# Layer norm in halves, products sorted by kind, earlier score blocks, and maxima negated where they are taken

## The chip, the cores and the metric

The kernel runs on one core of one Trainium2 chip. The metric is the device time of that core in microseconds (us); three runs of the kernel before gave 1825.66 to 1826.9 us, with a median of 1826.27 us.

## The reference

The input x is 2048 tokens of 512 numbers. It is normed, and the normed tokens go through an attention of 32 heads of width 16 and through a feed-forward net; the net's output gates the attention's. The weights wo and those of the net are drawn at random too.

```python
xn = (x - mean(x)) / sqrt(var(x) + 1e-5)
q, k, v = split(xn @ wqkv)                 # 32 heads of 16
p = softmax(q @ k.T * 16 ** -0.5)          # per head, 2048 x 2048
s = (p @ v) @ wo
g = silu(((xn @ w_gate) * (xn @ w_up)) @ w_down)
out = x + s * g
```

## The kernel before, in words

**Precision.** Every product is made of three: each operand is split into a high part in fp32r and a low part, and high times high, high times low and low times high are summed in one PSUM bank.

**Early stage** (`early`, up to 118.5 us). The 16 token tiles of 128 are normed in four chunks of four tiles. A chunk takes statistics on DVE (L161, L162), the root on DVE and ACT (L166, L167), six tiny DVE operations (L171 to L176) that give the scale e and the offset mr, the application (L183 on DVE for tiles 0 and 1, L185 on ACT for the others), and per tile a "turn": four PE transposes into one bank of tag "x" (L192), the high part copied out by ACT (L195), the low part subtracted on DVE (L196). POOL splits the weights wk and wq (L132 cast, L133 subtract) and subtracts the low parts of the V weights.

PE then works through a stream of 264 "products" (a product is one matmul with 512 columns; 12 make one result of k, q or v). The list `gens` gives their order: k of chunk 0, q of chunk 0, V tiles 0 and 1, k of chunk 1, and so on. A finished k or q bank is cast by ACT (L262), its low part is subtracted on DVE (L266), and both are stored to DRAM (KD, QD) and loaded again into `ks` and `qs` in the layout of the heads, all through the queue of SP. Results of k, q and V share two banks of tag "f". The table in `early` says at which product number each piece of the norm of chunks 1 to 3 is issued; the list EARLY says at which product numbers a score block stands. A score block is four matmuls s (L512) and four DVE maxima over 512 keys (L514), in four banks of tag "s". There are 21 of them.

**Rounds** (512, from 118.5 us on). A unit is four heads and 512 queries; it has 16 rounds of 128 keys. A round has four matmuls t (L538, scores with the row maximum subtracted, through two extra rows of `qs`), whose exponentials ACT takes (L540), four matmuls s with their maxima for the unit 21 rounds later (L512, L514), a portion of "filler" (projections, feed-forward net, last product), and the four pv matmuls of the round before (L549).

**Maxima.** When a unit's 64 partial maxima per row are there, `maxima` reduces them on DVE to m (L518), writes -m rounded to fp32r into one half of mm (L521), and two steps of the round's loop later (four steps make a round) writes the rest, -m minus that, into the other half (L524), transposes mm (L526) and sends it through DRAM (MD) into the two extra rows of `qs`. The unit's first t needs them; that is six rounds after `maxima`. There are 32 of them; the first is taken in the early stage, with no steps between.

**Order.** PE, ACT and DVE run in the order in which the program is written. POOL and the queue of SP are ordered by the scheduler.

Of the kernel before, what the change touches and what calls it, by code (L numbers as in the profile page):

```python
# [34 lines left out]
SPLIT_ROUNDS = 4  # L35
EBUFS = 12
HBUFS = 2
EARLY = [66 + 9 * n for n in range(21)]
EARLY_BUFS = {"s": 4, "x": 2, "f": 2}
BUFS = {"st": 2, "s": 3, "pv": 1, "misc": 2}  # L40
LOWER, UPPER = slice(0, 64), slice(64, P)
# [4 lines left out]
def body(ctx, tc, x, wqkv, wo, wg, wu, wd, out):  # L46
# [4 lines left out]
    def dma(dst, src):  # L51
        nc.sync.dma_start(dst, src)
# [45 lines left out]
    def soon(n, fn):  # L98

        if n:  # L100
            waiting.append((steps[0] + n, fn))
        else:
            fn()

# [20 lines left out]
    def wtile(name):  # L125
        return keep.tile([P, ND, P], F32 if name[-1] == "r" else F32R, name=name, bufs=1 if name[-1] == "r" else 2)

    def split(name, src):

        raw, hi, lo = [wtile(name + n) for n in "rhl"]  # L130
        dma(raw, src.rearrange("(d p) f -> p d f", p=P))
        nc.gpsimd.tensor_copy(hi, raw)  # L132
        nc.gpsimd.tensor_tensor(lo, raw, hi, op=OP.subtract)  # L133
        return hi, lo

# [16 lines left out]
    def load_x(tt):  # L152
        dma(tokens(tt), x[tt * P:(tt + 1) * P])

    def ln_stats(tt):
        c, t = divmod(tt, 4)
        if t == 0:
            norm[c] = [qp.tile([P, 4, 2], F32, name="mv", bufs=2)] + [qp.tile([P, 4], F32, name=n, bufs=2)
                                                                        for n in ("ve", "r0", "e1", "mr")]
        st = qp.tile([P, 6], F32, name="st", bufs=2)  # L160
        nc.vector.bn_stats(st, tokens(tt))  # L161
        nc.vector.bn_aggr(norm[c][0][:, t], st)  # L162

    def ln_root(c):
        mv, ve, r0, e, mr = norm[c]
        nc.vector.tensor_scalar(ve, mv[:, :, 1], 1e-5, None, op0=OP.add)  # L166
        nc.scalar.activation(r0, ve, AF.Sqrt)  # L167

    def ln_scale(c):
        mv, ve, r0, e, mr = norm[c]  # L170
        nc.vector.reciprocal(r0, r0)  # L171
        nc.vector.tensor_tensor(e, r0, r0, op=OP.mult)
        nc.vector.tensor_tensor(e, e, ve, op=OP.mult)
        nc.vector.tensor_scalar(e, e, -0.5, 1.5, op0=OP.mult, op1=OP.add)
        nc.vector.tensor_tensor(e, r0, e, op=OP.mult)
        nc.vector.scalar_tensor_tensor(mr, mv[:, :, 0], -1.0, e, op0=OP.mult, op1=OP.mult)  # L176

    def ln_apply(tt):
        c, t = divmod(tt, 4)
        mv, ve, r0, e, mr = norm[c]  # L180
        xt = tokens(tt)
        if tt < 2:
            nc.vector.tensor_scalar(xt, xt, e[:, t:t + 1], mr[:, t:t + 1], op0=OP.mult, op1=OP.add)  # L183
        else:
            nc.scalar.activation(xt, xt, AF.Identity, bias=mr[:, t:t + 1], scale=e[:, t:t + 1])  # L185

    def ln_turn(tt):
        c, t = divmod(tt, 4)
        xt = tokens(tt)
        pt = psum("x", f"xT{tt}")  # L190
        for d in range(ND):
            nc.tensor.transpose(pt[:, d * P:(d + 1) * P], xt[:, d * P:(d + 1) * P], ident)  # L192
        ptv = pt.rearrange("p (d q) -> p d q", d=ND)
        sl = slice(t * P, (t + 1) * P)
        nc.scalar.activation(xh[c][:, :, sl], ptv, AF.Copy)  # L195
        nc.vector.tensor_tensor(xl[c][:, :, sl], ptv, xh[c][:, :, sl], op=OP.subtract)  # L196


    def mm3(o, lh, ll, rh, rl, first, last):
        nc.tensor.matmul(o, lh, rh, start=first, stop=False)  # L200
        yield 1
        nc.tensor.matmul(o, lh, rl, start=False, stop=False)
        yield 1
        nc.tensor.matmul(o, ll, rh, start=False, stop=last)  # L204
        yield 2 if last else 1

    def terms(lh, ll, rh, rl, n):
        return [t for d in range(n) for t in ((lh(d), rh(d)), (lh(d), rl(d)), (ll(d), rh(d)))]
# [29 lines left out]
    def qk_proj(w, m, which, c, tag):  # L238
        wh, wl = w
        o = psum(tag, f"p{which}_{m}_{c}")  # L240
        for d in range(ND):
            yield from mm3(o, wh[:, d], wl[:, d], xh[c][:, d], xl[c][:, d], d == 0, d == ND - 1)
        qk_out(o, qk_high(o), m, which, c)

    def proj_pair(m, which):
# [30 lines left out]
    def v_proj(w, tt, tag):  # L276
        wh, wl = w
        c, t = divmod(tt, 4)
        sl = slice(t * P, (t + 1) * P)
        o = psum(tag, f"v{tt}")  # L280
        for d in range(ND):
            yield from mm3(o, xh[c][:, d, sl], xl[c][:, d, sl], wh[d], wl[d], d == 0, d == ND - 1)
        dst = V[:, tt, 0:H * VW].rearrange("p (h e) -> p h e", e=VW)[:, :, 0:DH]
        nc.scalar.activation(dst, o.rearrange("p (h e) -> p h e", e=DH), AF.Copy)  # L284

# [227 lines left out]
                         k[b:b + KB, pr, kc * 512:(kc + 1) * 512], start=True, stop=True)  # L513
        nc.vector.tensor_reduce(MX[i][:, j, t, kc:kc + 1], o, axis=AX.X, op=OP.max)  # L514

    def maxima(i, wait=2):
        m = keep.tile([P, 16], F32, name="m", bufs=2)
        nc.vector.tensor_reduce(m, MX[i].rearrange("p j t k -> p (j t) k"), axis=AX.X, op=OP.max)  # L518
        mm = keep.tile([P, 4, 2, 4], F32R, name="mm", bufs=2)
        m4 = m.rearrange("p (j t) -> p j t", t=4)  # L520
        nc.vector.tensor_scalar(mm[:, :, 0], m4, -1.0, None, op0=OP.mult)  # L521

        def rest():
            nc.vector.scalar_tensor_tensor(mm[:, :, 1], m4, -1.0, mm[:, :, 0], op0=OP.mult, op1=OP.subtract)  # L524
# [55 lines left out]
    def early():  # L580

        nc.scalar.activation(look, ones[0:1, 0:1], AF.Sqrt)
        for tt in range(4):
            load_x(tt)
        wk, wq = qk_weights(0, 1), qk_weights(0, 0)
        for tt in range(4, 8):
            load_x(tt)
# [3 lines left out]
        for tt in range(8, NT):  # L591
            load_x(tt)
        for tt in range(4):
            ln_stats(tt)
        ln_root(0)
        ln_scale(0)
        for tt in range(4):
            ln_apply(tt)
        for tt in range(4):
            ln_turn(tt)  # L600
        ones_rows(ks[0])
# [12 lines left out]

        def v(*tts):
            for tt in tts:
                yield from v_proj(wv, tt, "f")

        at = {n: [] for n in range(265)}
        for c, (stats, root, scale, apply, turns) in {1: ((0, 2, 4, 6), 8, 10, 14, (36, 48)),  # L620
                                                      2: ((26, 28, 30, 32), 34, 38, 40, (72, 84)),
                                                      3: ((50, 52, 54, 56), 58, 62, 64, (108, 120))}.items():
            for t, n in enumerate(stats):
                at[n].append((ln_stats, 4 * c + t))
            at[root].append((ln_root, c))
            at[scale].append((ln_scale, c))
            for t in range(4):
                at[apply].append((ln_apply, 4 * c + t))
                at[turns[t // 2]].append((ln_turn, 4 * c + t))
        at[turns[1] + 2] += [(ones_columns, slice(8, NT)), (other_keys, None)]  # L630
        scored = 0
        gens = [k(0), q(0), v(0, 1), k(1), q(1), v(2, 3), k(2), v(4, 5), k(3), v(*range(6, NT))]
        stream = (n for g in gens for n in g)
        for n in range(265):
            for fn, arg in at[n]:
                fn(arg)
            if n in EARLY:
                for _ in range(4):
                    r, j = divmod(scored, 4)
                    score(r // 16, r % 16, j)  # L640
                    scored += 1
                if scored == 64:
                    maxima(0, 0)
            next(stream, None)
        assert scored == 4 * LEAD
        return wq
# [124 lines left out]
```

## Time and profile before

| | |
|---|---|
| median of three runs | 1826.27 us |
| the profiled execution | 1826.91 us, of which the span is 1825.1 us |
| early stage, 0 to 118.5 us | PE busy 95.10, DVE 88.16, ACT 35.55, POOL 16.85 us |
| rounds, 118.5 to 1740 us | PE busy 1617.49 of 1621.50 us, DVE 1381.22, ACT 1152.52, POOL 502.66 |
| the last stretch, 1740 to 1825.1 us | PE busy 77.67 of 85.10 us |
| first product; first t | 17.89 us; 118.47 us |

Rows of the timeline read: start, duration, engine, line, operation, what it writes <- what it reads, sizes, count, and in brackets the idle time before it with what ended it. A matmul's duration is longer than its distance from the next one, since matmuls overlap: costs on PE are taken from starts. Rows of the chain read: start, duration, engine, tile, line. PEclk is the share of the full clock that TensorE was granted.

### The profile page before, as it was taken

The page shows a single profiled execution, that of the slowest core. Times are in us where ns is not written, and L with a number is a line of the kernel's source. Part 1 is how long each engine was busy: PE and PEld are TensorE (multiplying, and loading weights), DVE is VectorE, ACT ScalarE, POOL GpSimd, SP SyncE. Part 2 cuts the span into 40 slices and gives each one's busy share as a digit, 9 for nine tenths or more (in the row PEclk, how much of TensorE's full clock was granted, in tenths as well). Part 3 has the DMA queues.
Part 4 walks back from the last instruction along what each step waited for, and adds up shares of the span by engine and source line. Part 5 has one row for each costly group of instructions (what it writes and reads, how often), then busy time and mean ns, then how long its engine had stood idle before and what let it go on. Part 6 is the DMA issues. An engine that isn't in the chain of part 4 may idle for free.

```text
span 1825.1 us, 34151 instructions
## 1 busy us (share of the span) xinstructions
PE 1790.3 (98%) x13560; PEld 989.0 (54%) x13560; DVE 1495.3 (82%) x2498; ACT 1236.5 (68%) x2362; POOL 544.7 (30%) x583
## 2 busy tenths in 40 slices
PE   5999999999999999999999999999999999999998
PEld 4665555555555555555555555555555555555555
DVE  6878888888888888888888888888888888888832
ACT  4246676767776767777777777776767767767674
POOL 2012332431431325332232441431315323223341
PEclk9999999999999999999999999999999999999999
DMA  5515622620222122411115220421125111111242
GB/s 180 136 35 174 224 112 105 161 63 22 68 56 60 51 80 84 80 47 49 39 42 131 68 62 22 91 53 34 55 75 125 46 40 56 37 45 51 97 144 96
DMA packets 117228, 145.73 MB, mean 80 GB/s; under 512 B 12620, under 2 KB 74060, under 8 KB 114380
## 3 DMA queue, kind: packets, MB, share of 16 engines
q1 hardware_dynamic: 117068, 143.55, 27.5%
q8 instruction: 106, 1.74, 0.4%
q14 instruction: 54, 0.44, 0.1%
HBM read 95.94 MB, written 47.45 MB: 79 GB/s over the span
## 4 chain that ended last, share of the span: by engine, by line
PE 93%; DVE 4%; ACT 1%; DMA 1%; issue 0%; POOL 0%; SPq 0%; DVEq 0%; ACTq 0%
PE pv L549 27%; PE t L538 21%; PE s L512 11%; PE y L223 6%; PE u L223 5%; PE u L227 4%; PE g L223 4%; PE g L227 4%; PE y L227 3%; PE p L223 3%; DVE mx L514 1%; PE z L227 1%; PE p L227 1%; PE z L223 1%; PE v L200 1%; PE v L204 0%
## 5 line engine op out<-in xcount | busy, mean ns | idle before, releaser
L514 DVE TENSOR_REDUCE mx<-s 128x1 f32<-128x512 f32 x2048 | 1309.5, 683 | 243.0 <-PE s L512 138.5
L540 ACT ACTIVATE e<-t 128x512 f32<-128x512 f32 x2048 | 1112.0, 596 | 431.4 <-PE s L512 242.8
L512 PE MATMUL s<-ks,qs 48*128 48x512 f32 x2048 | 701.7, 427 | 4.9 <-DVE mx L514 3.1
L538 PE MATMUL t<-qs,ks 50*128 50x512 f32 x2048 | 704.8, 426 | 1.3 <-ACT V L284 0.7
L538 PEld LDWEIGHTS t<-qs,ks 50*128 50x128 f32 x2048 | 346.9, 185 | 500.7 <-ACT e L540 471.4
L549 PE MATMUL pv<-e,V 128*32 128x512 f32 x4096 | 545.7, 605 | 0.0
L512 PEld LDWEIGHTS s<-ks,qs 48*128 48x128 f32 x2048 | 337.6, 184 | 32.3 <-DVE mx L514 13.7
L132 POOL CAST w0h<-w0r 128x512 fp32r<-128x512 f32 x60 | 36.7, 612 | 468.3 <-PE u L223 351.4
L549 PEld LDWEIGHTS pv<-e,V 128*32 128x32 f32 x4096 | 81.0, 108 | 156.1 <-issue 147.0
L336 POOL CAST dh<-wdr 128x512 fp32r<-128x512 f32 x56 | 33.7, 613 | 292.6 <-PE y L227 157.5
L227 PE MATMUL u<-fh,w0h 64*128 64x512 f32 x224 | 88.3, 394 | 0.0
L227 PE MATMUL y<-dh,hh 64*128 64x512 f32 x224 | 88.1, 393 | 0.0
L223 PE MATMUL u<-fh,w0l 64*128 64x512 f32 x224 | 87.9, 393 | 0.0
L223 PE MATMUL g<-fh,w1l 64*128 64x512 f32 x224 | 87.8, 392 | 0.0
L223 PE MATMUL u<-fh,w0h 64*128 64x512 f32 x224 | 87.7, 392 | 0.0
L227 PE MATMUL g<-fl,w1h 64*128 64x512 f32 x224 | 87.7, 391 | 0.0
L223 PE MATMUL g<-fh,w1h 64*128 64x512 f32 x224 | 87.7, 391 | 0.0
L223 PE MATMUL g<-fl,w1h 64*128 64x512 f32 x224 | 87.6, 391 | 0.0
L227 PE MATMUL g<-fh,w1h 64*128 64x512 f32 x224 | 87.6, 391 | 0.0
L223 PE MATMUL u<-fl,w0h 64*128 64x512 f32 x224 | 87.6, 391 | 0.0
L223 PE MATMUL y<-dh,hh 64*128 64x512 f32 x224 | 87.5, 391 | 0.0
L223 PE MATMUL y<-dh,hl 64*128 64x512 f32 x224 | 87.5, 391 | 0.0
(248 smaller groups left out, 2890.7 us busy)
## 6 DMA issues: line engine op xcount, KB each, us to landing
w1r<-in_wg_dram SPq DMA_DIRECT2D x56, 256.0 KB
w0r<-in_wu_dram SPq DMA_DIRECT2D x56, 256.0 KB
wdr<-in_wd_dram SPq DMA_DIRECT2D x56, 256.0 KB
qs<-QD SPq DMA_DIRECT2D x64, 192.0 KB
ks<-KD SPq DMA_DIRECT2D x12, 768.0 KB
KD<-hl SPq DMA_DIRECT2D x16, 512.0 KB
QD<-hl SPq DMA_DIRECT2D x16, 512.0 KB
OD<-tr SPq DMA_DIRECT2D x31, 256.0 KB
```

The source lines that it names most:

```text
L132: nc.gpsimd.tensor_copy(hi, raw)
L200: nc.tensor.matmul(o, lh, rh, start=first, stop=False)
L223: nc.tensor.matmul(outs[k], l[LOWER], r[LOWER], start=k == 0 and n == 0, stop=(stop or k == 0) and n == len(low) - 1, skip_group_check=k == 1)
L227: nc.tensor.matmul(outs[1 - k], l[UPPER], r[UPPER], start=k == 0 and m == 0, stop=(stop or k == 0) and m == len(high) - 1, skip_group_chec ...
L336: nc.gpsimd.tensor_copy(dh[:, i], raw)
L512: nc.tensor.matmul(o, QS[i][b:b + KB, pr, t * P:(t + 1) * P], k[b:b + KB, pr, kc * 512:(kc + 1) * 512], start=True, stop=True)
L514: nc.vector.tensor_reduce(MX[i][:, j, t, kc:kc + 1], o, axis=AX.X, op=OP.max)
L538: nc.tensor.matmul(o, k[b:b + KR, pr, kt * P:(kt + 1) * P], QS[i][b:b + KR, pr], start=True, stop=True)
L540: nc.scalar.activation(e, o, AF.Exp, scale=DH ** -0.5)
L549: nc.tensor.matmul(fst["pv"][32 * j:32 * j + 32], V[:, kt, h0:h0 + 32], es[j], start=kt == 0, stop=kt == NT - 1)
```

## The change

1. Chunk 0 is normed in halves, tiles 0 and 1 first; only tile 2 is applied by DVE. The low parts of tiles 0 and 1 are subtracted after the second half's application, and the four turns use banks of tag "s". POOL's casts of wk and wq are made to wait for the application of tile 2. The loads of x tiles 4 to 7 move behind those of the V weights. PE gets six matmuls of `ident` by a tile of zeros whose result nobody reads ("warm"): four ahead of the first turn, one after two turns, one after four.
2. A result's twelve products are issued by kind: the four of high by high, then the four with the low part that comes from the weights, then the four with the low part of x.
3. The table of chunks 1 to 3 moves: statistics, root, scale and application come later, and tiles are turned one at a time between products. The third V tile comes ahead of k of chunk 1.
4. EARLY starts at product 44 instead of 66 and ends at 258 instead of 246.
5. `maxima` takes both m and its fp32r half by a negating DVE reduce (L532, L534), the other half by a subtraction on POOL (L535), and waits eight steps, two rounds, ahead of the transpose (L539) instead of two steps.

The core of the diff:

```diff
-EARLY = [66 + 9 * n for n in range(21)]
+EARLY = [44, 54, 64, 74] + [94 + 41 * n // 4 for n in range(17)]
...
+        cast = nc.gpsimd.tensor_copy(hi, raw)
+        if after is not None:
+            tc.add_manual_dep(cast.ins, after.ins.name, BEHIND, reason="keeps the port free for the layer norm")
...
-        if tt < 2:
+        if tt == 2:
...
-        pt = psum("x", f"xT{tt}")
+        norm["x", tt] = pt = psum("x" if c else "s", f"xT{tt}")
...
+        for k, (l, r) in enumerate(kinds):
+            for d in range(ND):
+                nc.tensor.matmul(o, l(d), r(d), start=k == d == 0, stop=k == 2 and d == ND - 1)
...
-    def maxima(i, wait=2):
-        m = keep.tile([P, 16], F32, name="m", bufs=2)
-        nc.vector.tensor_reduce(m, MX[i].rearrange("p j t k -> p (j t) k"), axis=AX.X, op=OP.max)
+    def maxima(i, wait=8):
+        m = keep.tile([P, 4, 4], F32, name="m", bufs=2)
+        nc.vector.tensor_reduce(m, MX[i], axis=AX.X, op=OP.max, negate=True)
         mm = keep.tile([P, 4, 2, 4], F32R, name="mm", bufs=2)
-        m4 = m.rearrange("p (j t) -> p j t", t=4)
-        nc.vector.tensor_scalar(mm[:, :, 0], m4, -1.0, None, op0=OP.mult)
+        nc.vector.tensor_reduce(mm[:, :, 0], MX[i], axis=AX.X, op=OP.max, negate=True)
+        nc.gpsimd.tensor_tensor(mm[:, :, 1], m, mm[:, :, 0], op=OP.subtract)
 
         def rest():
-            nc.vector.scalar_tensor_tensor(mm[:, :, 1], m4, -1.0, mm[:, :, 0], op0=OP.mult, op1=OP.subtract)
             mt = keep.tile([P, 32], F32, name="mt", bufs=2)
...
+        def warm(n):
+            for _ in range(n):
+                nc.tensor.matmul(psum("f", "warm"), ident, on.rearrange("p b e -> p (b e)"), start=True, stop=True)
+
+        warm(4)
+        first = (0, 1), (2, 3)
...
-        for c, (stats, root, scale, apply, turns) in {1: ((0, 2, 4, 6), 8, 10, 14, (36, 48)),
-                                                      2: ((26, 28, 30, 32), 34, 38, 40, (72, 84)),
-                                                      3: ((50, 52, 54, 56), 58, 62, 64, (108, 120))}.items():
+        for c, (stats, root, scale, apply, turns) in {1: ((0, 2, 4, 6), 13, 16, 18, (34, 38, 42, 46)),
+                                                      2: ((50, 52, 54, 56), 58, 60, 62, (78, 81, 84, 88)),
+                                                      3: ((92, 96, 100, 104), 106, 108, 110, (114, 118, 122, 126))}.items():
...
-        gens = [k(0), q(0), v(0, 1), k(1), q(1), v(2, 3), k(2), v(4, 5), k(3), v(*range(6, NT))]
+        gens = [k(0), q(0), v(0, 1, 2), k(1), q(1), v(3), k(2), v(4, 5), k(3), v(*range(6, NT))]
```

Three places show what moves. On PE, the first score block before: it stands in the last third of q of chunk 1 (`p_0_1`; the names give line, operation, what is written <- what is read, and the size).

```order
L200 MATMUL p_0_1_470<-xh_149,w0h 128x512
L202 MATMUL p_0_1_470<-xl_153,w0h 128x512
L204 MATMUL p_0_1_470<-xh_149,w0l 128x512
L512 MATMUL s_0_0_487<-ks_132,qs 128x512
L512 MATMUL s_0_1_490<-ks_132,qs 128x512
```

On PE in the changed program it stands in the second V tile (`e` holds the V weights, `fh` and `fl` the parts of chunk 0, `ks_133` x tiles 4 to 7, `xT` a turn).

```order
L218 MATMUL v_367<-e,fl 128x512 x2
L218 MATMUL v_388<-e,fh 128x512 x2
L202 MATMUL xT_391<-ident,ks_133 128x128 x4
L218 MATMUL v_388<-e,fh 128x512 x4
L202 MATMUL xT_402<-ident,ks_133 128x128 x4
L218 MATMUL v_388<-e,fh 128x512 x2
L526 MATMUL s_0_0_411<-ks_132,qs 128x512
L526 MATMUL s_0_1_414<-ks_132,qs 128x512
```

The block has moved ahead of all of k and q of chunk 1, and the turns now stand alone between products. The second place is DVE at the scale of chunk 3, before (`r` and `e` are the root and the scale, `hl` the parts of k of chunk 1).

```order
L166 TENSOR_SCALAR ve<-mv 128x4
L266 TENSOR_TENSOR hl<-p_0_1_431,hl 128x512
L171 RECIPROCAL r_436<-r_436 128x4
L172 TENSOR_TENSOR e_437<-r_436 128x4
L173 TENSOR_TENSOR e_437<-e_437,ve 128x4
L174 TENSOR_SCALAR e_437<-e_437 128x4
L175 TENSOR_TENSOR e_437<-r_436,e_437 128x4
L176 SCALAR_TENSOR_TENSOR mr<-mv,e_437 128x4
L514 TENSOR_REDUCE mx<-s_0_0_487 128x1
```

And on DVE in the changed program, where six score blocks stand ahead of it.

```order
L172 BN_STATS st<-V 128x6
L173 BN_AGGR mv<-st 128x2
L528 TENSOR_REDUCE mx<-s_5_0_636 128x1
L528 TENSOR_REDUCE mx<-s_5_1_639 128x1
L528 TENSOR_REDUCE mx<-s_5_2_642 128x1
L528 TENSOR_REDUCE mx<-s_5_3_645 128x1
L177 TENSOR_SCALAR ve<-mv 128x4
L183 RECIPROCAL r_595<-r_595 128x4
L184 TENSOR_TENSOR e_596<-r_595 128x4
```

The scale of chunk 3 has moved from ahead of the first block's maxima to behind those of the sixth block. The third place is DVE at the maxima of a unit in the rounds, before.

```order
L514 TENSOR_REDUCE mx<-s_15_2_2337 128x1
L518 TENSOR_REDUCE m<-mx 128x16
L521 TENSOR_SCALAR mm<-m 128x4x4
L514 TENSOR_REDUCE mx<-s_0_1_2352 128x1
L514 TENSOR_REDUCE mx<-s_0_0_2359 128x1
L524 SCALAR_TENSOR_TENSOR mm<-m,mm 128x4x4
L526 STREAM_TRANSPOSE mt<-mm 128x32
```

The same place on DVE in the changed program.

```order
L528 TENSOR_REDUCE mx<-s_15_2_2362 128x1
L532 TENSOR_REDUCE m<-mx 128x16
L534 TENSOR_REDUCE mm<-mx 128x4x4
L528 TENSOR_REDUCE mx<-s_0_1_2378 128x1
L528 TENSOR_REDUCE mx<-s_0_0_2385 128x1
L528 TENSOR_REDUCE mx<-s_0_3_2400 128x1
L528 TENSOR_REDUCE mx<-s_0_2_2407 128x1
L528 TENSOR_REDUCE mx<-s_1_1_2418 128x1
L528 TENSOR_REDUCE mx<-s_1_0_2425 128x1
L528 TENSOR_REDUCE mx<-s_1_3_2440 128x1
L528 TENSOR_REDUCE mx<-s_1_2_2447 128x1
L539 STREAM_TRANSPOSE mt<-mm 128x32
```

Two operations on m have left DVE, one reduce has come, and the transpose stands behind eight maxima instead of two. On POOL the subtraction of unit 30 stands here in the changed program (`w0l` is a low part of the attention's output, whose raw part comes by a load).

```order
L385 CAST w0h<-w0r 128x512
L150 TENSOR_TENSOR fl<-wdr,fh 128x512
L386 TENSOR_TENSOR w0l<-w0r,w0h 128x512
L535 TENSOR_TENSOR mm<-m,mm 128x4x4
L385 CAST hl<-w1r 128x512
```

The subtraction takes its turn behind whatever POOL has ahead of it there; the other POOL rows keep their order.

More of the change, by code (lines that the diff above doesn't have):

```diff
@@ L101, in soon @@
             waiting.append((steps[0] + n, fn))
+            waiting.sort(key=lambda w: w[0])
         else:
@@ L178, in ln_apply, with ln_turn, ln_low, full @@
     def ln_apply(tt):
-        c, t = divmod(tt, 4)
-        mv, ve, r0, e, mr = norm[c]
+        (mv, ve, r0, e, mr), t = norm[tt]
         xt = tokens(tt)
-        if tt < 2:
[L183 to L187, printed above, removed]
+        if tt == 2:
+            return nc.vector.tensor_scalar(xt, xt, e[:, t:t + 1], mr[:, t:t + 1], op0=OP.mult, op1=OP.add)
+        return nc.scalar.activation(xt, xt, AF.Identity, bias=mr[:, t:t + 1], scale=e[:, t:t + 1])
+    def ln_turn(tt, low=True):
         c, t = divmod(tt, 4)
         xt = tokens(tt)
-        pt = psum("x", f"xT{tt}")
+        norm["x", tt] = pt = psum("x" if c else "s", f"xT{tt}")
         for d in range(ND):
             nc.tensor.transpose(pt[:, d * P:(d + 1) * P], xt[:, d * P:(d + 1) * P], ident)
-        ptv = pt.rearrange("p (d q) -> p d q", d=ND)
-        sl = slice(t * P, (t + 1) * P)
[L195 to L205, printed above, removed]
+        nc.scalar.activation(xh[c][:, :, t * P:(t + 1) * P], pt.rearrange("p (d q) -> p d q", d=ND), AF.Copy)
+        if low:
+            ln_low(tt)
+    def ln_low(tt):
+        c, t = divmod(tt, 4)
+        sl = slice(t * P, (t + 1) * P)
+        nc.vector.tensor_tensor(xl[c][:, :, sl], norm["x", tt].rearrange("p (d q) -> p d q", d=ND), xh[c][:, :, sl],
+                                op=OP.subtract)
+    def full(o, kinds):
+        for k, (l, r) in enumerate(kinds):
+            for d in range(ND):
+                nc.tensor.matmul(o, l(d), r(d), start=k == d == 0, stop=k == 2 and d == ND - 1)
+                yield 1
     def terms(lh, ll, rh, rl, n):
@@ L240, in qk_proj @@
         o = psum(tag, f"p{which}_{m}_{c}")
-        for d in range(ND):
-            yield from mm3(o, wh[:, d], wl[:, d], xh[c][:, d], xl[c][:, d], d == 0, d == ND - 1)
+        hi, lo = [lambda d, w=w: w[:, d] for w in (wh, wl)]
+        yield from full(o, ((hi, lambda d: xh[c][:, d]), (lo, lambda d: xh[c][:, d]), (hi, lambda d: xl[c][:, d])))
         qk_out(o, qk_high(o), m, which, c)
@@ L280, in v_proj @@
         o = psum(tag, f"v{tt}")
-        for d in range(ND):
-            yield from mm3(o, xh[c][:, d, sl], xl[c][:, d, sl], wh[d], wl[d], d == 0, d == ND - 1)
+        hi, lo = [lambda d, x=x: x[c][:, d, sl] for x in (xh, xl)]
+        yield from full(o, ((hi, lambda d: wh[d]), (hi, lambda d: wl[d]), (lo, lambda d: wh[d])))
         dst = V[:, tt, 0:H * VW].rearrange("p (h e) -> p h e", e=VW)[:, :, 0:DH]
@@ L584, in early @@
             load_x(tt)
-        wk, wq = qk_weights(0, 1), qk_weights(0, 0)
-        for tt in range(4, 8):
-            load_x(tt)
+        wraw = []
+        for which in (1, 0):
+            wraw.append(wtile(f"w{which}r"))
+            dma(wraw[-1], wqkv[:, which * D:which * D + P].rearrange("(d p) f -> p d f", p=P))
         raws = [etile() for _ in range(ND)]
@@ L590, in early @@
             dma(raws[d], wqkv[d * P:(d + 1) * P, 2 * D:])
-        for tt in range(8, NT):
+        for tt in range(4, NT):
             load_x(tt)
[L593 to L597, printed above, removed]
-            ln_apply(tt)
-        for tt in range(4):
-            ln_turn(tt)
-        ones_rows(ks[0])
+        def warm(n):
[3 more added lines that the diff above has]
+        first = (0, 1), (2, 3)
+        for tts in first:
+            ln_open(tts)
+        ln_stats(0)
+        ln_stats(1)
+        ln_root(first[0])
+        ln_stats(2)
+        ln_scale(first[0])
+        for tt in first[0]:
+            ln_apply(tt)
+        ln_stats(3)
+        ln_root(first[1])
+        ln_turn(0, False)
+        ln_turn(1, False)
+        warm(1)
+        ln_scale(first[1])
+        last = ln_apply(2)
+        ln_apply(3)
+        ln_low(0)
+        ln_low(1)
+        ln_turn(2)
+        ln_turn(3)
+        warm(1)
+        wk, wq = [split_raw(f"w{which}", raw, last) for which, raw in zip((1, 0), wraw)]
         wv = [[etile().bitcast(F32R) for _ in range(ND)] for _ in range(2)]
```

51 lines of the change are left out of this document (30 added, 21 removed).

## The prediction

> **What bounds the kernel now.** I read the page, then the busy time by stage, the chain of waits, and the timeline where the change acts. The page's head and its chain by engine:
>
> ```profile
> span 1825.1 us, 34151 instructions
> PE 93%; DVE 4%; ACT 1%; DMA 1%; issue 0%; POOL 0%; SPq 0%; DVEq 0%; ACTq 0%
> ```
>
> Busy time by stage (stretch, its length, busy PE, PEld, DVE, ACT, POOL, granted clock, DMA share, GB/s):
>
> ```profile
> 0.00:118.50 118.50, 95.10 (x414) 65.25 (x414) 88.16 (x172) 35.55 (x62) 16.85 (x26) 0.97 0.48 135
> 118.50:1740.00 1621.50, 1617.49 (x12588) 876.71 (x12588) 1381.22 (x2287) 1152.52 (x2206) 502.66 (x533) 1.00 0.26 74
> ```
>
> PE is the bound: in the rounds it is idle for 4 us of 1621.5. The change removes none of its work there, so only places where something else sets the pace can give time: the early stage (23.4 us of idle PE) and the maxima, where DVE's 4% of the chain lies. The profiled run took 1826.91 us, 0.64 above the median of 1826.27; I make the sum against it and take 0.64 off at the end.
>
> **1. The start.** The timeline of the first norm:
>
> ```profile
> 5.72 0.69 DVE L161 BATCH_NORM_STATS2 st<-ks 128x6 f32<-128x512 f32 x1 [0.59 <-DMA ks<-in_x_dram]
> 8.97 1.26 POOL L133 TENSOR_TENSOR w1l<-w1r,w1h 128x512 fp32r<-128x512 f32 x1
> 9.05 1.20 DVE L173 TENSOR_TENSOR e<-e,ve 128x4 f32<-128x4 f32 x1
> 10.29 1.33 DVE L174 TENSOR_SCALAR e<-e 128x4 f32<-128x4 f32 x1
> 17.89 0.47 PE L200 MATMUL p<-fh,w1h 128*128 128x512 f32 x1 [0.78 <-ACT fh L195]
> 23.43 0.16 DVE L173 TENSOR_TENSOR e<-e,ve 128x4 f32<-128x4 f32 x1
> ```
>
> L173 takes 0.16 us at 23.43 but 1.20 at 9.05, where it ends as POOL's subtraction does; L174 behind it takes 1.33, beside POOL's second one. The change moves these POOL operations behind the application, and the first half needs only two statistics, which are done when the third tile lands (5.72). Six scale operations of 0.2 after the third statistics give mr at about 7.7, two ACT applications of 0.75 the first turn at about 9.2, the last high copy at 13.0 and the first product at 13.1: **-4.8 us**. A warm matmul should take 1.0 us at full clock (as the pv of a round, quoted below) and twice that at half; four fill PE from 2.4 to 9.2 and delay nothing as long as the clock rises on the way. If it doesn't, the first turn slips by up to 1.5 us, and the first product, which waits for POOL's cast of wk and the fourth turn, by less.
>
> **2. The stream of products.** The prices (timeline), and PE's waits in the early stage:
>
> ```profile
> 45.32 0.39 PE L202 MATMUL p<-xl,w0h 128*128 128x512 f32 x1
> 45.55 0.40 PE L204 MATMUL p<-xh,w0l 128*128 128x512 f32 x1
> 46.86 0.40 PE L202 MATMUL p<-xl,w0h 128*128 128x512 f32 x1
> 46.95 2.48 DVE L514 TENSOR_REDUCE mx<-s 128x1 f32<-128x512 f32 x4
> ```
> ```profile
> PE p L200 <- ACT xh L195: 4.3, 1, 4.3
> PE xT L192 <- DVE xl L196: 1.7, 1, 1.7
> PE s L512 <- DMA ks<-KD: 1.1, 2, 0.6
> PE v L200 <- DVE hl L266: 0.8, 1, 0.8
> ```
>
> A product costs 0.23 us; the block between 45.55 and 46.86 costs 1.31 less two products, 0.85; its four maxima hold DVE for 2.48. Work on PE is the same before and after. Waits of 0.8, 1.7 and 4.3 us all come from turns and banks of chunks 0 and 1, which come earlier now: **-6.8**.
>
> New waits come in their place. The first block needs q of chunk 0 back from DRAM:
>
> ```profile
> 24.23 2.93 ACT L185 ACTIVATE ks<-ks,mr,e 128x512 f32<-128x512 f32 x4 [1.34 <-DVE mr L176]
> 27.07 0.57 ACT L262 ACTIVATE hl<-p 128x512 fp32r<-128x512 f32 x1
> 28.40 0.80 SPq L55 DMA_DIRECT2D QD<-hl  x2
> 32.27 0.78 SPq L55 DMA_DIRECT2D qs<-QD  x2
> 55.76 0.79 SPq L55 DMA_DIRECT2D qs<-QD  x2
> ```
> ```profile
> DMA  9931111110000360299999999567200000000000
> ```
>
> The last line is DMA activity from 55 to 60 us in fortieths: the load issued at 55.76 moves data until 58.6, so it takes 2.9. From the second store's issue (28.8) to the load's issue (32.27) pass 3.5 us, at the later turn (52.84 to 55.76) 2.9; a round trip takes 5.8 to 6.4. The cast of q stood behind four applications, and does again: the norm of chunk 1 is ready at about 20.4, ACT is through at 23.3, the low part of q at 24.6. So V tile 1 (product 36) waits 2.5 us for q's bank, and the first block, with its store at 24.6 and 25.0, has its keys at 31.2. PE reaches product 44 at 27.6: **a wait of 3.65 us**, where before there was none (45.88 was reached with data long there). New waits: +2.5 and +3.65.
>
> Chunk 3: PE goes through block 6 (product 104, at 57.8) and ten products to product 114 at 60.7. DVE has the fifth block's maxima until about 57.2, three statistics (0.8 each), the sixth block's maxima (2.5), root and scale (1.7), and ACT an application: turn 12 can start at 64.9, **+4.3**. Turn 10 waits 1.1 in the same way. Blocks 64 and 74 stand closer (ten products, 2.3 us, and a block, 0.85) than with turns before, DVE needs 2.5 for each plus the turns' low parts, and PE waits 1.8 for banks, as long as blocks 84, 93 and 129 waited by the same bookkeeping before.
>
> The clock, over stretches of about 3.4 us:
>
> ```profile
> 33.90:37.30 3.40, 0.63 (x5) 0.39 (x4) 0.82 (x6) 2.38 (x4) 0.00 (x0) 1.00 0.39 78
> 37.40:40.70 3.30, 1.78 (x3) 1.12 (x4) 2.30 (x5) 1.90 (x4) 0.00 (x0) 0.50 0.00 0
> ```
>
> After a stretch with 0.63 us of work the clock was halved, for two such stretches; that cost about 2.2 us. The gap of 3.65 us is like that one, if it covers most of a stretch, so I keep one halving, at 2.6 us: +0.4. [...]
>
> Keys of chunk 3:
>
> ```profile
> 83.52 5.36 DMA ks<-KD
> ```
>
> Here the load took 5.36 us instead of 2.9, as eight loads for the second group's keys ran beside it. In the new order some of those go out earlier, and the block stands two products later: about -1.3 (the 1.1 us of the waits above and a little). Against it a contended store would cost 0.8 at the block of product 94, whose keys land just in time.
>
> Early stage: -4.8 - 6.8 + 2.5 + 3.65 + 4.3 + 1.1 + 0.4 - 1.3 + 0.8 = -0.15, so **-0.2 us**: first t at 118.3 instead of 118.47. The unsure terms are the reloads (bounds 0 and +5.4) and the clock (-2.6).
>
> **3. Maxima.** The reduce m of all 32 (shortest, median, longest in ns), a held L521 with POOL beside it, then the chain's rows of held ones (the first and the last of seven in the rounds; the eighth, at 1740.5, is the last unit's):
>
> ```profile
> L518 DVE TENSOR_REDUCE m<-mx x32: 219/220/221, 100.9 to 1740.3; 128x16 f32<-128x64 f32 x32
> ```
> ```profile
> 1105.58 1.30 POOL L133 TENSOR_TENSOR w1l<-w1r,w1h 128x512 fp32r<-128x512 f32 x1
> 1105.84 1.07 DVE L521 TENSOR_SCALAR mm<-m 128x16 fp32r<-128x16 f32 x1
> ```
> ```profile
> 367.38 0.79 DVE mm L521
> 369.36 1.29 DVE mm L524
> 1633.27 1.06 DVE mm L521
> ```
>
> L521 normally takes 0.17; here it ends when POOL's subtraction does. L518, a reduce of the same kind as the new L534, never takes more than 0.221, beside POOL or not. So L521's 1.06 becomes 0.22. What the round gains is seen from its pv starts in the chain, held and not held:
>
> ```profile
> 1100.32 0.99 PE pv L549 x8
> 1108.05 1.00 PE pv L549 x8
> 1163.12 0.99 PE pv L549 x8
> 1170.17 1.00 PE pv L549 x8
> ```
>
> Two rounds take 7.73 us with a held one and 7.05 without: 0.7 lost. Six such: 4.2. At 367 both L521 and L524 are held: 0.57 + 1.29 = 1.9. The one at 1740 I take at 0.7. Together **-6.8**. Where L521 isn't held, DVE has 0.22 for 0.17 and later saves L524 (0.16); PE covers both: nothing.
>
> The subtraction on POOL: the nearest rows bound it by 0.2 (small memset) and 1.3 us (512 columns). It has two rounds (about 6.6 us from the maxima) until the transpose wants it, and POOL's row ahead ends within 2.5 us of the maxima in 30 of 32 units. In unit 30 it doesn't (its first reduce, and POOL's row):
>
> ```profile
> 1685.69 0.22 DVE L518 TENSOR_REDUCE m<-mx 128x16 f32<-128x64 f32 x1
> ```
> ```profile
> 1692.31 1.30 POOL L372 TENSOR_TENSOR w0l<-w0r,w0h 128x512 fp32r<-128x512 f32 x1
> ```
>
> This ends 7.9 us after the maxima; the transpose waits 1.6, and all maxima and h products behind it on DVE with it: +0.7 (bounds 0 and 1.6). The eight steps' wait delays MD by about 5 us; the unit's t come some 16 us after the maxima, so the chain to `qs` (2 us and a load) stays hidden. If that cover went, a unit would lose the DMA's excess, under 1 us. Rounds: **-6.1**.
>
> **Sum.** 1826.91 - 0.2 - 6.1 = 1820.6; less 0.64: **1820.0 us**.
>
> **Rivals.** For C, a row of POOL's waits (total, times, longest):
>
> ```profile
> POOL dh L336 <- PE y L223: 99.9, 4, 37.4
> ```
>
> A. The forecast, 0.47.
> B. The reloads of the early stage run as slow as the one at 83.52, 2.4 to 2.7 us more for the first block, or for it and that at product 94: first t at 120.5 to 123.8, total 1822 to 1825.5. For it: x tiles and weights still arrive at the start. Against it: by 25 us these are in. 0.15.
> C. Slower: the transpose on DVE waits for POOL's subtraction, which stands behind a POOL instruction that itself waits for PE. POOL does wait for PE so, 99.9 us in four waits. It decides where POOL's row ahead ends later than 6.6 us after the maxima. One row that waits for a whole portion of the filler, at the longest single wait of 37.4 us, would cost 37.4 - 6.6, about 30 us: 1850. Against it: I laid the new POOL order beside the old times, and only unit 30 is late. 0.06.
> D. The clock stays full in the first block's gap: 2.6 us less, 1817.4. 0.27.
> E. The second reduce is held by POOL as L521 was, so that the change doesn't take the stall away: L524's 1.3 alone goes, about 1825. Against it: L518's constant 0.22. 0.05.
>
> **Range and chances.** 0.2% is 3.65 us, about what a measurement of this kernel tells from no change. A lies at 1818 to 1823, D at 1815.5 to 1819.5, B at 1822 to 1825.5: 1815 to 1825.5 leaves out C, half of E and the tails. Faster than 1822.6: 0.42 of A, all of D, 0.03 of B, 0.72. Slower than 1829.9: C, 0.06. The same: 0.22.
>
> **What would show it.** Right: first product near 13, the first block's s idle for 3 to 4 us on the load of qs, a turn idle some 4 us at chunk 3, first t near 118; no negating reduce over 0.25 us, the round at each former held place back at 3.5. Wrong: two or more transposes (L539) that wait on POOL's subtraction, a first t after 121, or a halved clock that lasts more than two stretches.

## The result and the profile after

The changed kernel takes 1828.66 us (median of 20 runs, 1825.74 to 1833.67), the kernel before 1826.62 us (20 runs, 1825.08 to 1828.38). The ratio is 1.0013, with a 95% interval of 1.0006 to 1.0020: a little slower. The forecast was 1820.0 us, with a range from 1815 to 1825.5; both the sign and the range were wrong.

Busy time by stage of the changed kernel, in the columns of before, and its chain by engine:

```profile
0.00:118.50 118.50, 105.79 (x422) 70.25 (x423) 85.24 (x175) 36.67 (x63) 17.00 (x27) 0.91 0.46 135
118.50:1740.00 1621.50, 1619.35 (x12619) 883.90 (x12617) 1374.48 (x2265) 1155.55 (x2213) 509.97 (x565) 1.00 0.26 74
1740.00:1827.00 87.00, 76.15 (x535) 46.39 (x533) 22.20 (x34) 45.59 (x89) 23.24 (x23) 0.94 0.33 110
```
```profile
PE 94%; DVE 2%; DMA 2%; issue 1%; POOL 1%; ACT 1%; SPq 0%; ACTq 0%; DVEq 0%; POOLq 0%
```

DVE's share of the chain has halved, as meant; DMA's has doubled. In the early stage PE is busy for 105.79 us instead of 95.10, with six idle matmuls more and a granted clock of 0.91 instead of 0.97. At a granted 0.5 the same matmuls last longer: two of a V tile's took 1.22 us at 34.55, where it was 0.5, and 0.71 at 28.73, where it was 1.00. In the last stretch the clock is 0.94.

Where the 1.9 us between the spans (1825.1 and 1827.0) come from is read from three marks: the first t, and the first reduce of the maxima of units 30 and 31. The rows of the kernel before for the first t and unit 31 (that of unit 30 stands in the prediction), then those of the changed kernel:

```profile
118.47 0.49 PE L538 MATMUL t<-qs,ks 50*128 50x512 f32 x1 [0.69 <-ACT V L284]
...
1740.29 0.22 DVE L518 TENSOR_REDUCE m<-mx 128x16 f32<-128x64 f32 x1
```
```profile
120.00 0.47 PE L551 MATMUL t<-qs,ks 50*128 50x512 f32 x1 [0.79 <-ACT V L298]
...
1680.73 0.22 DVE L532 TENSOR_REDUCE m<-mx 128x16 f32<-128x64 f32 x1
...
1736.45 0.22 DVE L532 TENSOR_REDUCE m<-mx 128x16 f32<-128x64 f32 x1
```

| stretch | before | after | change | forecast |
|---|---|---|---|---|
| to the first t | 118.47 | 120.00 | +1.5 | -0.2 |
| to the maxima of unit 30 (1685.69; 1680.73) | 1567.2 | 1560.7 | -6.5 | -6.1 |
| to those of unit 31 (1740.29; 1736.45) | 54.6 | 55.7 | +1.1 | +0.7 |
| to the end | 84.8 | 90.5 | +5.7 | -0.7 |

The rounds gave what was forecast. The early stage lost instead of staying even, and the last unit took back nearly all.

**The start.** The first half's scale is no longer held, and the product that was first at 17.89 stands here:

```profile
6.97 0.16 DVE L185 TENSOR_TENSOR e<-e,ve 128x2 f32<-128x2 f32 x1
7.17 0.17 DVE L186 TENSOR_SCALAR e<-e 128x2 f32<-128x2 f32 x1
...
13.12 0.70 PE L218 MATMUL p<-fh,w1h 128*128 128x512 f32 x2
```

**PE's waits in the early stage** (total, times, longest):

```profile
PE xT L202 <- ACT V L195: 3.8, 1, 3.8
PE s L526 <- DMA qs<-QD: 3.1, 1, 3.1
...
PE v L218 <- DVE hl L280: 2.2, 1, 2.2
```

These are the three new waits of the prediction: 4.3, 3.65 and 2.5 were forecast. What the forecast lacked is in the clock. Five stretches, each ahead of a halving of the clock (length, then busy PE; PEclk is that of the stretch itself, the next one ran at 0.5):

```profile
21.38:24.79 3.41, 1.13 (x6) 0.69 (x6) 0.60 (x1) 3.41 (x7) 0.00 (x0) 1.00 0.43 115
28.20:31.60 3.40, 1.25 (x8) 0.71 (x6) 0.86 (x2) 0.60 (x1) 0.00 (x0) 1.00 0.40 100
45.27:48.68 3.41, 3.06 (x10) 1.38 (x9) 2.34 (x4) 3.40 (x5) 0.00 (x0) 1.00 0.00 0
62.34:65.75 3.41, 0.58 (x3) 0.14 (x1) 2.97 (x12) 0.74 (x2) 0.00 (x0) 1.00 0.00 0
1751.90:1755.30 3.40, 0.66 (x8) 0.00 (x0) 2.49 (x4) 0.76 (x2) 1.93 (x2) 1.00 0.67 217
```

The clock was halved four times in the early stage, for 3.41, 6.83, 3.41 and 6.83 us, 20.5 us together; before, once, for 6.83 us.

**The last unit.** The queue of SP around its maxima, before:

```profile
1741.77 0.53 SPq L52 DMA_DIRECT2D w0r<-OD  x1
1742.35 0.56 SPq L52 DMA_DIRECT2D MD<-mt  x1
1747.19 0.58 SPq L52 DMA_DIRECT2D w1r<-OD  x1
1747.82 0.74 SPq L52 DMA_DIRECT2D qs<-MD  x2
```

The same in the changed kernel, then POOL's operation that frees w0r there, and the t that needs the rows:

```profile
1743.25 0.57 SPq L52 DMA_DIRECT2D w1r<-OD  x1
1746.41 0.57 SPq L52 DMA_DIRECT2D w0r<-OD  x1
1747.04 0.93 SPq L52 DMA_DIRECT2D out_dram<-dl  x2
1748.06 0.56 SPq L52 DMA_DIRECT2D MD<-mt  x1
1748.67 0.66 SPq L52 DMA_DIRECT2D dl<-in_x_dram  x1
1752.38 0.33 SPq L52 DMA_DIRECT2D dl<-YD  x1
1752.75 0.66 SPq L52 DMA_DIRECT2D qs<-MD  x2
```
```profile
1745.11 1.27 POOL L386 TENSOR_TENSOR w0l<-w0r,w0h 64x512 fp32r<-64x512 f32 x1
```
```profile
1756.31 1.03 PE t L551 x2
```

The transpose was done at 1741.0, but MD's store now stands behind a second load of w0r, which has to wait until POOL has read the first (1746.38), and behind the output's store; the load of `qs` stands behind a load into dl, which has to wait for that output's store. MD's store is issued 7.2 us after the transpose started (1740.84), the load of `qs` 11.9; the chain has the output's store at 4.78 us and t idle for 3.75. The clock is halved for the 6.83 us that follow. So a DMA that nothing in its own data delays was late because of its place in the queue.

**Maxima.** The new reduce of all 32 (shortest, median, longest in ns), the former held place at 1105 by its pv starts, and the transposes of units 30 and 31:

```profile
L534 DVE TENSOR_REDUCE mm<-mx x32: 206/208/213, 103.8 to 1736.6; 128x16 fp32r<-128x64 f32 x32
```
```profile
1098.17 0.99 PE pv L562 x8
1101.68 0.99 PE pv L562 x8
1105.10 0.99 PE pv L562 x8
```
```profile
1688.90 0.24 POOL L535 TENSOR_TENSOR mm<-m,mm 128x16 fp32r<-128x16 f32 x1
...
1689.17 0.21 DVE L539 STREAM_TRANSPOSE mt<-mm 128x32 f32<-128x32 f32 x1 [2.32 <-POOL mm L535]
```

No second reduce is held. The two rounds at the held place take 6.93 us instead of 7.73. In unit 30 the transpose waits 2.32 us for POOL's subtraction, which stands where it was expected to stand; the round there takes 4.73 us instead of 3.51.

### The profile page after: what moved, and what is told of

It is laid out like the page before. It is cut to its first block, busy times and chain, and to the rows that moved or that the text cites. A ratio compares the mean times of both kernels' runs of the same rounds, so it can differ in the third digit from the quotient of the medians.

```text
span 1827.0 us, 34170 instructions
## 1 busy us (share of the span) xinstructions
PE 1801.3 (99%) x13572; PEld 1000.5 (55%) x13572; DVE 1481.9 (81%) x2472; ACT 1237.8 (68%) x2364; POOL 550.2 (30%) x615
## 4 chain that ended last, share of the span: by engine, by line
PE 94%; DVE 2%; DMA 2%; issue 1%; POOL 1%; ACT 1%; SPq 0%; ACTq 0%; DVEq 0%; POOLq 0%
PE pv L562 27%; PE t L551 21%; PE s L526 11%; PE y L237 6%; PE u L237 5%; PE g L237 4%; PE u L241 4%; PE g L241 4%; PE p L237 3%; PE y L241 2%; PE v L218 2%; PE z L237 1%; PE z L241 1%; PE p L241 1%; DVE mx L528 1%
```

## The experiments

The theory after the result was: the new maxima and the new early stage are separate; the last unit's place in SP's queue costs 5.8 us, unit 30's subtraction 1.6, and the early stage loses by waits that DVE's and ACT's order sets and by the halvings that follow such waits. The rivals stand with each run. Medians are of all runs of a kernel, ratios to the kernel before on the same chip (its medians there were 1825.96 and 1826.13); they are estimated from all runs and differ a little from the quotient of the medians. A first t is read from one profile of each kernel. Where two kernels share the early stage it still differed by 2.6 us (120.00 and 122.64) and by 3.4 us (116.33 and 112.93), so a difference of about 3 us between two profiles says little by itself.

### The last unit waits two steps

```diff
-                maxima(si)
+                maxima(si, 2 if si == NU - 1 else 8)
```

> The changed kernel, but the last unit's maxima wait two steps as before, all others eight. Theory (the late transpose lets the scheduler put the last unit's MD behind a load of w0r that waits for POOL and behind a load of dl that waits for the output's store): the 5.8 us of the two rounds at 1751 to 1764 go, 1828.7 becomes about 1823, and no clock halving is left near 1755. Rival (the last unit is late because the output's transfers collide there, wherever MD stands in the queue): 1828.7, the t of the last unit still waits 4 to 5 us on its load.

1822.90 us, ratio 0.9984 (0.9975 to 0.9994). MD's store is back ahead of the loads:

```profile
1742.21 0.53 SPq L52 DMA_DIRECT2D w0r<-OD  x1
1742.80 0.55 SPq L52 DMA_DIRECT2D MD<-mt  x1
1747.37 0.58 SPq L52 DMA_DIRECT2D w1r<-OD  x1
1748.01 0.74 SPq L52 DMA_DIRECT2D qs<-MD  x2
```

No t waits for it: PE's longest wait from 1740 to 1770 us is 0.2. The 5.8 us are gone with one number changed. That number also makes the transpose itself 2.7 us earlier (1.65 us after the maxima instead of 4.39), but in the changed kernel MD's store was issued 7 us after the transpose was done, behind the rows shown above: the place in the queue is the cause. The order of the queue is the scheduler's; how it decides is not shown, only that six steps were enough to move the store past three others. (This run's early stage was worse, first t at 122.64 us, with another 2.3 us of waits for keys.)

### The new maxima in the kernel before

The function `maxima` of the changed kernel in the kernel before, with the changed kernel's line that keeps waiting steps sorted; nothing else.

```diff
-    def maxima(i, wait=2):
+    def maxima(i, wait=8):
...
-        nc.vector.tensor_scalar(mm[:, :, 0], m4, -1.0, None, op0=OP.mult)
+        nc.vector.tensor_reduce(mm[:, :, 0], MX[i], axis=AX.X, op=OP.max, negate=True)
+        nc.gpsimd.tensor_tensor(mm[:, :, 1], m, mm[:, :, 0], op=OP.subtract)
```

> The kernel before, with the new maxima alone (two negating reduces, the subtraction on POOL, eight steps), early stage untouched. Theory (each held place in the rounds gains 0.6 to 1.0, 4.7 us together, unit 30's wait for POOL costs 1.6, the last unit's late MD 5 to 6): 1 to 3 us slower than before, 1827 to 1829, with unit 30 and the last unit late in the trace. Rival (the last unit's delay needs the shift of the early stage): 3 to 5 us faster than before, 1821 to 1823.

1827.77 us, ratio 1.0005 (0.9996 to 1.0014). The queue of SP and PE's waits in the last 80 us of it:

```profile
1744.71 0.57 SPq L52 DMA_DIRECT2D w0r<-OD  x1
1745.34 1.41 SPq L52 DMA_DIRECT2D out_dram<-dl  x2
1746.84 0.57 SPq L52 DMA_DIRECT2D MD<-mt  x1
...
1751.01 0.59 SPq L52 DMA_DIRECT2D qs<-MD  x2
```
```profile
PE t L538 <- DMA qs<-MD: 3.5, 1, 3.5
PE s L513 <- DVE mx L515: 0.6, 1, 0.6
```

The late MD and unit 30's wait (its transpose waits 2.1 us for POOL) come with the new maxima alone, whatever the early stage. By itself that part of the change is worth nothing measurable: what the rounds gain goes at the end.

### The changed kernel with the old maxima

The function `maxima` of the kernel before in the changed kernel; nothing else.

```diff
-    def maxima(i, wait=8):
+    def maxima(i, wait=2):
...
-        nc.vector.tensor_reduce(mm[:, :, 0], MX[i], axis=AX.X, op=OP.max, negate=True)
-        nc.gpsimd.tensor_tensor(mm[:, :, 1], m, mm[:, :, 0], op=OP.subtract)
+        nc.vector.tensor_scalar(mm[:, :, 0], m4, -1.0, None, op0=OP.mult)
```

> The changed kernel with the maxima as before, so that the early stage's change stands alone. Theory (the early stage as changed loses 1 to 2 us, more where the clock is halved more often, and touches nothing later): 1826.5 to 1829, the held places back, no late MD in the last unit. Rival (the early stage as such is no loss, and the profile of the changed kernel was an unlucky one): 1824 to 1826.

1829.80 us, ratio 1.0013 (1.0003 to 1.0022), first t at 122.56; the time is a little above what was expected. The old maxima are held as before:

```profile
L535 DVE TENSOR_SCALAR mm<-m x32: 174/175/1215, 106.4 to 1744.7; 128x16 fp32r<-128x16 f32 x32
```

No t waits in the last unit. The early stage as changed is a loss of its own, by 1.5 to 4.2 us in the three profiles that have it (first t at 120.00, 122.64, 122.56, beside 118.47 and 118.40 in the two profiles with the early stage of before).

### The blocks at their old products

```diff
-EARLY = [44, 54, 64, 74] + [94 + 41 * n // 4 for n in range(17)]
+EARLY = [66 + 9 * n for n in range(21)]
```

> The changed kernel with the score blocks at their old product numbers, 66 to 246. Theory (the first block's wait for q's round trip, and DVE's maxima ahead of the norm of chunk 3, are the early stage's loss): no wait for qs at the first block, the turn of chunk 3 waits about 2 us instead of 3.8, first t at 110 to 112 instead of 120, total about 1820. Rival (the loss is the clock's, and comes with whatever gaps are left): first t at 117 to 120, total 1826 to 1829.

1821.93 us, ratio 0.9981 (0.9972 to 0.9990), with the late MD still in it. No block waits for q, the turn of chunk 3 waits 1.9 us, but the first t comes at 116.33, not at 110 to 112. The waits went as expected, but the clock was halved three times, for 13.7 us, at 24.9 (V tile 1's wait for q's bank), at 59.0 and at 86.3 (the granted clock was 0.94 over the first 118.5 us); what that is worth is taken up with the mended kernel below, which has the same early stage and half as much half clock. The stretch ahead of the second halving had this much work:

```profile
55.61:59.02 3.41, 2.25 (x7) 0.91 (x6) 2.90 (x11) 0.74 (x2) 0.00 (x0) 1.00 0.00 0
```

### The two gaps filled

```diff
         for n in range(265):
+            if n in (44, 114):
+                for _ in range(3):
+                    nc.tensor.matmul(psum("s", "warm"), ident, on.rearrange("p b e -> p (b e)"), start=True, stop=True)
```

> The changed kernel with three more idle matmuls each ahead of product 44 and of product 114, so that PE works in the two longest gaps. Theory (the clock is halved because of these gaps): no halving at 31.6 and at 65.8 us; each took up to 3.4 us of work, so first t at 114 to 117 and a total of 1823 to 1826. Rival (the halvings come from the many short waits in the stretches limited by DVE): halvings as before, first t at 119 to 121, total 1828 to 1829.

1827.10 us, ratio 1.0002 (0.9993 to 1.0011); first t at 117.06. Two halvings of 3.41 us are left, at 25.9 and at 46.4 (the granted clock was 0.97 over the first 118.5 us, and 1.00 from 63.5 to 66.9); those behind the two filled gaps are gone, though PE does no useful work in them and the waits last as long. The first t came at the late end of what was expected and the total a little above it. Beside the changed kernel's profile (first t at 120.00, 13.7 us more of half clock) it puts the price of that half clock at about 3 us; this is one profile against one, and no more than profiles of one early stage differ by.

### Blocks, last unit and unit 30 mended

The old EARLY, two steps for the last unit, and in `maxima`:

```diff
-        nc.gpsimd.tensor_tensor(mm[:, :, 1], m, mm[:, :, 0], op=OP.subtract)
+        (nc.vector if i == NU - 2 else nc.gpsimd).tensor_tensor(mm[:, :, 1], m, mm[:, :, 0], op=OP.subtract)
```

> The changed kernel with the old product numbers of the blocks, two steps for the last unit, and the subtraction of unit 30 on DVE. Theory: the gains add up, 8 to 10 us of the early stage, 5.8 of the last unit and 1.6 of unit 30: 1811 to 1814. Rival (the rounds are bound by PE so that what is taken away early comes back as waits): 1818 to 1823.

1816.45 us, ratio 0.9941 (0.9924 to 0.9957); the expected 1811 to 1814 was missed by a few us. Unit 30 and the last unit no longer wait (PE's longest wait from 1640 to 1760 us is 0.2), and the first t comes at 112.93. The early stage is that of the run with the blocks at their old products, so the two profiles price the clock too. Between the first product and the first t PE waits 7.5 us in both; there the clock is halved for 13.65 us and the stretch takes 103.11 us, here for 6.83 us and 100.32. That is 2.8 us for 6.8 us of half clock, about twice the price that the run with the gaps filled gave, and would account for the later first t there. The profiled run of 1821.57 lost 7 us at one place near 360 us: POOL had a row of weight splits behind late loads of wdr, and the product h waited for it.

```profile
PE u L241 <- DVE h L346: 2.2, 1, 2.2
```
```profile
359.14:362.55 3.41, 1.80 (x13) 0.55 (x5) 0.45 (x2) 2.02 (x4) 3.33 (x5) 1.00 0.67 167
```

After that stretch the clock was halved for 10.24 us; over the whole profiled run it was 0.994 of the full one. This is the place of the held L521 and L524 at 367 in the kernel before. Its round takes 4.1 to 8.0 us in seven of the profiles with the new maxima, against 3.5 undisturbed; in the changed kernel's own and in the one without the idle matmuls it takes 3.7 and 3.6. With the old maxima in the changed kernel it takes 6.0. So the 1.9 us that were put down to held operations there belong in part to POOL's backlog, which stays.

### The norm ahead of the blocks

On top of the mended kernel, blocks at 70 + 9n, and the table moved:

```diff
-EARLY = [66 + 9 * n for n in range(21)]
+EARLY = [70 + 9 * n for n in range(21)]
...
-        {1: ((0, 2, 4, 6), 13, 16, 18, (34, 38, 42, 46)),
-         2: ((50, 52, 54, 56), 58, 60, 62, (78, 81, 84, 88)),
-         3: ((92, 96, 100, 104), 106, 108, 110, (114, 118, 122, 126))}
+        {1: ((0, 2, 4, 6), 13, 16, 26, (34, 38, 42, 46)),
+         2: ((28, 30, 32, 34), 38, 40, 50, (78, 82, 86, 90)),
+         3: ((54, 56, 58, 60), 64, 66, 92, (114, 118, 122, 126))}
```

> The mended kernel with blocks at 70 + 9n, the application of chunk 1 behind the cast of q of chunk 0, and statistics, root and scale of chunks 2 and 3 ahead of the first block's maxima. Theory (all waits of the early stage are orders on DVE and ACT): no wait of PE over 1.3 us between the first product and the first t, first t at 102 to 105, no or one halved window, total 1804 to 1810. Rival (loads, or PSUM banks, set the pace whatever the order): first t at 109 to 113, total 1813 to 1818.

1804.14 us, ratio 0.9880 (0.9865 to 0.9894). PE's three longest waits up to the first t, and the stage:

```profile
PE warm L610 <- POOL on L83: 2.4, 1, 2.4
PE s L526 <- DMA ks<-KD: 0.9, 2, 0.6
PE t L551 <- ACT V L298: 0.7, 1, 0.7
```
```profile
0.00:101.60 101.60, 96.45 (x424) 64.57 (x424) 85.45 (x177) 36.86 (x64) 17.01 (x27) 1.00 0.56 157
```

First t at 101.61, a little earlier than expected, and once full, the clock is not halved before the last 2.7 us of the program (granted 1.00 over the first 101.6 us, 0.999 over the whole run). The theory is borne out: nearly all waits of the early stage went with the orders on DVE and ACT; the 0.9 us on keys are what is left of waits for loads. This kernel beats both.

### Without the idle matmuls

The kernel with the norm ahead, and `warm` issuing nothing.

```diff
-            for _ in range(n):
+            for _ in range(0):
```

> The kernel of the run before without the six idle matmuls. Theory (they raise the clock some 8 us earlier; without them turns and the first products run at half clock until about 17 us): the first products 1 to 2 us later, first t 1 to 3 us later than there, total 1 to 3 us more. Rival (the first product waits for the weights' cast and the copies, and half clock is covered): no difference.

1805.69 us, ratio 0.9883 (0.9868 to 0.9898): no difference that the runs can tell. The clock rises at 12.1 us instead of 7.3, the first product comes at 13.22 instead of 12.63, and the first t at 101.64 instead of 101.61. The rival was right: half clock at the start is covered by the weights' splits (the first product's own wait is 0.78 us on POOL's w1l). What takes up the 0.6 us between there and the first t is not shown.

### The table alone

The changed kernel with the table of the norm ahead (its three lines, as in the diff two runs above) and nothing else; blocks still from 44 on.

```diff
-        {1: ((0, 2, 4, 6), 13, 16, 18, (34, 38, 42, 46)),
+        {1: ((0, 2, 4, 6), 13, 16, 26, (34, 38, 42, 46)),
...
```

> The changed kernel with the table of the norm's pieces alone as in the kernel with the norm ahead; blocks stay at 44 to 258, the last unit's maxima at eight steps. Theory (the norm's place on DVE and ACT is worth 4 to 5 us of PE's waits and two of the halvings, the first block's wait for q stays at 3 to 4 us with its halving): first t at 108 to 112. Rival (the place of the blocks is what counts): first t at 117 or later.

One run, first t at 115.68 us (120.00 with the change's own table), total 1824.31 beside 1827.19 for one run of the kernel before. Both were off. The turns wait 0.7 us at most, instead of 3.8, but the blocks, now not held up, run into the keys:

```profile
PE s L526 <- DMA ks<-KD: 4.3, 4, 3.1
PE s L526 <- DMA qs<-QD: 3.0, 2, 2.5
```

The blocks alone give 3.7 to 7.1 us of the early stage (116.33, and 112.93 in the mended kernel), the table alone 4.3 (115.68), both together, with the blocks four products later yet, 18. What the four products give by themselves was not run.

## Why the prediction was wrong, point by point

1. **Start, -4.8.** Right: 13.12 us for a forecast 13.1, behind the last high copy (done at 12.97 for a forecast 13.0). The idle matmuls were cheaper than forecast, 0.86 us at full clock and 1.7 at half for 1.0 and 2.0, and the clock rose at 7.72, before the first turn.
2. **Products.** The waits that went, and the three new ones, were right in place and within 0.55 us in size (2.2, 3.1 and 3.8 for 2.5, 3.65 and 4.3). The 1.1 us at turn 10 and the 0.8 at the block of product 94 did not come.
3. **"I keep one halving, at 2.6 us".** This failed. The clock was halved four times, for 20.5 us. Rival D, a clock that stays full in the first block's gap, had 0.27 and would have made the time shorter; the run went the other way: the clock was halved in that gap, from 31.62 us on, and the stretches ahead of three of the four halvings had 0.17 to 0.37 of their time at work (0.58, 1.13 and 1.25 of 3.4 us). The first t came 1.7 us later than forecast (120.0 for 118.3), although the waits were 3.25 us less than forecast (1.35 shorter, 1.9 that did not come). These 5 us or so stand against 13.7 us more of half clock, whose price the runs put between 3 us (gaps filled) and, as an estimate from the two profiles with one early stage, 5.6. So the clock can account for them, at the upper end of its price; a run that shows it alone is missing.
4. **Maxima, six held places at 0.7.** Right, from 0.6 to 1.0 in the trace; L534 is never held (at most 0.213 us, though 8 of the 32 lie within a two-input operation of POOL), which settles rival E. **The place at 367, 1.9:** the profiled run gained 2.1, but seven other runs keep 0.6 to 4.5 us there: a wrong reading of a chain in which POOL's backlog stood as well. **The last unit's 0.7:** 0.1, its round being long for another reason.
5. **Unit 30, +0.7 (bounds 0 and 1.6).** Right in mechanism, and between the forecast and its upper bound: the round takes 4.73 instead of 3.51 us, and the stretch from these maxima to the next unit's is 1.1 us longer.
6. **"The chain to `qs` (2 us and a load) stays hidden. If that cover went, a unit would lose the DMA's excess, under 1 us".** This is the step that turned the sign. It counted how late the transpose would be, but not where the scheduler would then put MD's store and load in SP's queue: behind a load that waits for POOL and behind one that waits for a store. The loss was 5.7 us, with 3.75 of idle PE and a halved clock behind it. The readings ahead of the run show the order of POOL in the changed program, and none of SP's queue. Rival C looked for such a thing on POOL, with the right form (a small step behind an instruction that waits) and on the wrong queue.

## What to carry to other kernels

A step that is moved takes its DMAs along: where a scheduler orders a queue, read the changed queue from the moved DMA upwards, and ask of each row above it what it waits for. On an engine that runs in the order of the program, as DVE does here, the norm of a later chunk belongs ahead of the reduces of earlier blocks if PE needs it before them; moving the blocks forward without it brings waits, and a wait costs more than its length where half clock follows it, as it did here for 3.41 or 6.83 us at a time. A round that is long at a held operation is not long because of it until the chain has been read to the other engine's backlog.

## What the runs showed of the hardware

In the early stage of the changed kernel the granted clock changed at 24.79, 28.20, 31.62, 38.44, 48.68, 52.10, 65.75 and 72.58 us: 3.41, 3.41, 6.83, 10.24, 3.41, 13.65 and 6.83 us from one change to the next, which is one, two, three or four times the shortest of them, within 0.02 us. In the kernel before it was halved there once, from 37.35 to 44.18 us, for 6.83.

PE's busy share of the 3.41 us ahead of a halving was 0.17 in the kernel before (33.94 to 37.35 us), 0.33, 0.37, 0.90, 0.17 and 0.19 in the five rows of the changed kernel above, 0.66 in the row 55.61:59.02 of the run with the blocks at their old products and 0.53 in the row 359.14:362.55 of the mended kernel. In the kernel before the clock stayed full behind 16.87 to 20.29 us with a share of 0.72 and behind 30.53 to 33.94 us with 0.51. So shares that kept the clock and shares that lost it overlap in these rows. The 0.90 is the row 45.27:48.68. The busy share may say too much there: the four matmuls of its score block start 0.6 us apart and are each recorded with 0.49 us, where a product costs 0.23. By an estimate that gives each matmul of that stretch 0.23 us from its start, PE was at work for 1.8 of 3.41 us, a share of 0.53. None of these eight stretches that lost the clock was idle throughout; at the end of the kernel before, one was (1819.11 to 1822.53 us, followed by half clock).

The first halving of the early stage began at 24.79 us in the changed kernel, at 24.9 with the blocks at their old products and at 25.9 with the gaps filled, with the same wait of 2.2 us for q's bank in all three. The changed kernel, with many gaps, spread over 7.9 us in 20 runs, the kernel before over 3.3; that the gaps make the difference is likely but not shown.

Beside a subtraction of POOL two operations on DVE of the kernel before took far longer than their medians: L521 up to 1.23 us instead of 0.17, L524 up to 1.35 instead of 0.17, both on 16 columns. A reduce of 64 elements was never longer than 0.221 us, in 32 cases of L518 before and 32 of L534 after. POOL's subtraction of 16 columns took 0.21 to 0.24 us, the low bound of the prediction.
